# Retention followed by a maxout feed-forward layer: the attention steps of a pair of chunks one part sooner, and a queue of vector steps popped at two more places

## The chip, the cores and the metric

One core of a Trainium2 chip runs the whole program. The metric is the device time of one execution in microseconds (us), lower is better; the median of three runs is compared.

## What is computed

The kernel computes retention (attention without softmax, with a decay by distance) for 8 batches, 8 heads, 576 positions and head size 64, and feeds its output, seen as 4608 rows of 512, into a feed-forward layer whose hidden value is the largest of three products:

```python
scores = scale * np.matmul(q, k.transpose(0, 1, 3, 2))
Dmat = np.where(rel >= 0, gamma[:, None, None] ** rel[None, :, :], 0.0)
attn_out = np.matmul(scores * Dmat[None], v)
x = np.ascontiguousarray(attn_out.transpose(0, 2, 1, 3)).reshape(B * S, H * D)
h = np.maximum(np.maximum(x @ w1, x @ w2), x @ w3)      # 512 -> 768
return (h @ w_out).astype(np.float32)                    # 768 -> 512
```

All arithmetic of the matrix products is fp32. The weights arrive as 64-bit floats and are converted on the chip in the first 120 us.

## The kernel before

**Tiles and chunks.** The 4608 rows are cut into 36 chunks of 128 rows; four chunks make a tile of 512 rows, so there are nine tiles, t = 0 to 8. Retention is done chunk by chunk with a running state. While TensorE does the feed-forward layer of tile t (`ffn(t)`), the retention of the four chunks of tile t+1 is laid between its products.

**The feed-forward part.** For t of 1 and more, `up` (line 550) does one block of 128 hidden features as 20 products of 128x128 by 128x256 (`PRODUCTS`), each on a sum of blocks of x and of weights; six blocks make 120 products a tile. They gather in five PSUM chains A to E. ScalarE copies the chains to SBUF (`part`, line 564) and VectorE joins the copies (line 559), 14 joins a block. The sums of x (`X_SUMS`, 13 VectorE steps, tiles named `s`, line 344) must be there before the products that read them. Then `downs` (line 406) does seven products of six matmuls each (names `dx`, `dy`, `dz`), with four stores: after the second, fifth, sixth and seventh product. The store's tile `osb` has two buffers.

**The retention steps of a chunk g.** `load(g)` (line 199) issues 32 small DMAs for q and k in blocks of 32 and two large ones for k and v, all from SyncE's queue. `transposes(g)` (line 217) are two VectorE transposes to kT and qT. `decay_values(g)` (line 209) is one GpSimd multiply of v (tile `vd`). `scores` (line 233) is 16 matmuls, masked by two VectorE multiplies (`st`). `values([a, b], [b, next])` (line 281) is the products of the masked scores with vd, then `state` of the two chunks named second (tile `kv`, of raw k and vd), then the products with the older state; its `output` (line 320) is two VectorE multiplies into xT, and on a tile's last pair the 13 `X_SUMS`. `keep` (line 263) makes the next state, one VectorE and one GpSimd step.

**What sets the order.** The order of every engine's instructions is written out by hand. Tile t's work is cut into twelve parts: `ffn` gives way after 14, 27, 40, 54, 67, 80, 94, 107 and 120 of its 120 products, and in `downs` after the second and the fourth product and at the end. `steps(t + 1)` lists what is put ahead of part 0 to 11; a pair of chunks takes six parts, the first pair from m = 0 and the second from m = 6. TensorE and GpSimd steps stand where they are called. VectorE steps and loads go through `soon` into the deque `urgent`, from which `chore` pops one at a time: in `ffn`, after every product with an odd number within its block (lines 646 and 647), four after each product of `downs` (line 660), and all that is left at the start of `scores` and `values` and at the end of the ups. A second deque, `chores`, holds sums of weights, in t = 1 alone.

The pools that hold the loads have two buffers for the small q and k tiles and for v, three for raw k, so a load of chunk g+2 overwrites what the transposes and the decay of chunk g have read.

Of the kernel before, what the change touches and what calls it, by code (L numbers as in the profile page):

```python
# [79 lines left out]
def kernel(  # L80
# [74 lines left out]
    for r in sorted({start_of(g) for g in range(NG)} - {0, None}):  # L155
        m = masks[r] = const.tile([C, C], FP32, name=f"causal{r}")
# [17 lines left out]
    def chore(n=1):  # L174
        for _ in range(n):
            if urgent or chores:
                (urgent or chores).popleft()()  # L177
# [198 lines left out]
    def sums_of_outs():  # L376

        pool = late["pool"]
        lo, hi = slice(0, DM // 2), slice(DM // 2, DM)
        b11, b12, b21, b22 = (w_out[:, :, e, r] for e in range(2) for r in (lo, hi))  # L380
        t1, t2, t4 = (pool.tile([P, NF // 2, DM // 2], FP32, name=f"To{n}")[:] for n in (1, 2, 4))

        def on_vector(fp):
            nc.vector.tensor_tensor(t1[:, fp], b12[:, fp], b11[:, fp], op=ALU.subtract)
            nc.vector.tensor_tensor(t2[:, fp], b22[:, fp], t1[:, fp], op=ALU.subtract)

        def on_gpsimd(fp):
            nc.gpsimd.tensor_tensor(b12[:, fp], b22[:, fp], b12[:, fp], op=ALU.subtract)
            nc.gpsimd.tensor_tensor(t4[:, fp], b21[:, fp], t2[:, fp], op=ALU.subtract)

        for fp in range(NF // 2):
            chores.extend([partial(on_vector, fp), partial(on_gpsimd, fp)])
        late["T"] = {1: b11, 2: b21, 3: b22, 4: t4, 5: t1, 6: t2, 7: b12}
        late["S"] = {n: pool.tile([P, NF // 2, NH], FP32, name=f"H{n}") for n in (1, 2, 3, 4)}
# [135 lines left out]
    def weight_sums(fp):  # L530

        def step(dst, a, sign, b):
            combine(*(factor(n, slice(2 * fp, 2 * fp + 2)) for n in (dst, a, b)), sign)

        for dst, _, a, sign, b in W_SUMS:
            chores.append(partial(step, dst, a, sign, b))
        chores.append(partial(summed_fp.add, fp))

    def late_room():
        pool = late["pool"]  # L540
        late["W"] = [pool.tile([P, NF, P], FP32, name=f"n{n}") for n in range(1, 9)]
        late["X"] = {n: pool.tile([P, NH], FP32, name=n)[:] for n in sorted({x[0] for x in X_SUMS})}
# [3 lines left out]
    def convert(n):  # L546
        for _ in range(n):
            next(converting, None)
# [35 lines left out]
    def downs_plain(t, h):  # L584

        ps = [(ps_x, ps_y)[m % 2].tile([P, DM], FP32, tag="xy"[m % 2], name="down") for m in range(NT // P)]
        for fb in range(NF):
            for m, b in enumerate(ps):
                nc.tensor.matmul(b[:], lhsT=h[:, fb, m * P:(m + 1) * P], rhs=w_sb["out", fb],  # L589
                                 start=(fb == 0), stop=(fb == NF - 1))  # L590
                if fb == NF - 1:
                    osb = opool.tile([P, DM], FP32, tag="osb", name="osb")
                    nc.scalar.copy(osb[:], b[:])
                    nc.sync.dma_start(out[t * NT + m * P:t * NT + (m + 1) * P, :], osb[:])
            yield

    def up_plain(t, h, fb, i):
        ps = (ps_x, ps_y)[fb % 2].tile([P, NT], FP32, tag="xy"[fb % 2], name="up")
        for dc in range(NDC):
            nc.tensor.matmul(ps[:], lhsT=w_sb[i, fb][:, dc * P:(dc + 1) * P], rhs=xT[t][:, dc, :],  # L600
                             start=(dc == 0), stop=(dc == NDC - 1))
        if i > 0:
            return lambda: nc.vector.tensor_tensor(h[:, fb, :], h[:, fb, :], ps[:], op=ALU.max)
        return lambda: nc.scalar.copy(h[:, fb, :], ps[:])

    def ffn(t):

        h = hpool.tile([P, NF, NT], FP32, tag="h", name="h")
        if t == 0:
            for fp, i in units:  # L610
                for fb in (2 * fp, 2 * fp + 1):
                    maximum = up_plain(t, h, fb, i)
                    convert(4)
                    maximum()
                yield
            convert(6)
            for fb, _ in enumerate(downs_plain(t, h)):
                convert(4 if fb < 2 else 4 * len(pieces))
                if fb == 2:
                    while_converting.close()  # L620
                    late["pool"] = ctx.enter_context(tc.tile_pool(name="late", bufs=1))
                    late_room()
                    sums_of_outs()
                elif fb > 2:
                    chore(2)
                if fb in (1, 3):
                    yield
            yield
            return
        if t == 1:  # L630
            spread.append(True)
            weight_sums(0)
            weight_sums(2)
        plain = (2, 3) if t == 1 else ()
        order = (2, 3, 0, 1, 4, 5) if t == 1 else (0, 1, 4, 5, 2, 3)
        total = sum(24 if fb in plain else len(PRODUCTS) for fb in order)
        count = parts = 0
        for n, fb in enumerate(order):
            if fb not in plain:
                while fb // 2 not in summed_fp:  # L640
                    chore()
            steps_of_one = up_plain_all(t, h, fb) if fb in plain else up(t, h, fb)
            for step, cost in enumerate(steps_of_one):
                if fb in plain:
                    chore(8)
                elif step % 2:
                    chore(len(urgent) > 0)
                elif step % 4 == 2 and chores:
                    chores.popleft()()
                count += cost or 1  # L650
                if count * (NF // 2 * 3) >= (parts + 1) * total:
                    parts += 1
                    yield
            if n % 2:
                sums_of_hidden(h, fb // 2)
                if fb in plain:
                    weight_sums(fb // 2)
        chore(len(urgent))
        for n, _ in enumerate(downs(t, h)):
            chore(4)  # L660
            if n in (1, 3):
                yield
        yield

    def up_plain_all(t, h, fb):
        for i in range(3):
            up_plain(t, h, fb, i)()
            yield 8
# [46 lines left out]
    def steps(t):  # L715


        todo = [[] for _ in range(3 * CPT)]

        def at(n, *what):  # L720
            for step, *args in what:
                if step is values:
                    if args[0][0] < NG:
                        todo[n].append(partial(values, args[0], [g for g in args[1] if g < NG]))
                elif args[0] < NG:
                    todo[n].append(partial(soon, partial(step, *args)) if step is load else partial(step, *args))

        if t == 1:
            a, b, c, d = range(CPT, 2 * CPT)
            at(0, (load, b))  # L730
            at(1, (scores, a), (state, a), (keep, a))
            at(2, (transposes, b), (decay_values, b), (load, c))
            at(3, (scores, b), (load_blocks, d, 0))
            at(4, (decay_values, c), (load_blocks, d, 1, 2))
            at(5, (values, [a, b], [b, c]), (load_blocks, d, 3), (load, d))
            at(6, (keep, c), (transposes, c), (load_blocks, d + 1, 0))
            at(7, (transposes, d), (decay_values, d), (load_blocks, d + 1, 1, 2))
            at(8, (scores, c), (scores, d), (load_blocks, d + 1, 3), (load, d + 1))
            at(9, (load_blocks, d + 2, 0, 1))
            at(10, (decay_values, d + 1), (load_blocks, d + 2, 2))  # L740
            at(11, (values, [c, d], [d, d + 1]), (load_blocks, d + 2, 3), (load, d + 2),
               (transposes, d + 1))
            return todo
        for n in range(0, CPT, 2):
            a, b, m = CPT * t + n, CPT * t + n + 1, 6 * (n // 2)
            at(m, (keep, a), (transposes, b), (decay_values, b))
            if a == 2 * CPT:
                at(m, (load, a + 2))
            at(m, (load, b + 2))
            at(m + 2, (scores, a), (scores, b))  # L750
            at(m + 4, (decay_values, a + 2))
            at(m + 5, (values, [a, b], [b, a + 2]), (transposes, a + 2), (load, a + 4))
        return todo

    for t in range(N // NT):
# [56 lines left out]
```

## Time and profile before

| | |
|---|---|
| time, median of 3 runs | 788.36 us (788.1 to 789.76) |
| profiled run | 786.77 us, its span on the core 785.1 us |
| tile 0 with the conversion of weights | from 27.8 to about 120 us |
| tile 1 | about 120 to 211.9 us |
| tiles 2 to 7 | 82 to 84 us each; they start at 211.9, 295.4, 377.7, 461.8, 544.2 and 628.6 us |
| tile 8, without retention beside it | from 711.4 us to the end |
| granted TensorE clock | 1.00 in all stretches |

The times of a stage are read from the timeline, where each row is a run of like instructions: start, length, engine and line, output from inputs. In this trace an fp32 matmul shows as two records, so "x2" of 128x256 is one product. A row's length is the modelled busy time, which reaches into the next row; the distance between the starts of two rows is the pace.

### The profile page before, as it was taken

How to read it: one execution, taken by the hardware profiler on the slowest of the kernel's cores; microseconds unless marked ns; L12 is line 12 of the kernel's file. 1: busy time of each engine (PE TensorE's matmuls, PEld its weight loads, DVE VectorE, ACT ScalarE, POOL GpSimd, SP SyncE). 2: the span in 40 equal slices, each digit the busy share in tenths (PEclk: the TensorE clock that was granted, in tenths of full speed). 3: DMA queues.
4: the chain of work that ended last, by engine and by line, in shares of the span. 5: the costliest groups of instructions: out<-in, count | busy, mean ns of one | idle time of the engine just before them, and what ended most of it. 6: DMA issues, size and time to landing. Idle time of an engine off the chain costs nothing.

```text
span 785.1 us, 14443 instructions
## 1 busy us (share of the span) xinstructions
PE 770.2 (98%) x5000; PEld 624.6 (80%) x5000; DVE 559.6 (71%) x1248; ACT 326.2 (42%) x808; POOL 100.5 (13%) x124
## 2 busy tenths in 40 slices
PE   8999999999999999999999999999999999999998
PEld 7545454688888888888788888888888888888887
DVE  2998979989486829693877567773869296937672
ACT  3664631243154504452354325432545044524651
POOL 2110012111010211010101111110012100200000
PEclk9999999999999999999999999999999999999999
DMA  9995543323313332333333333333133423101001
GB/s 219 228 236 128 156 110 101 58 46 58 94 27 63 76 81 46 56 60 55 92 56 58 58 94 58 58 57 98 27 62 62 93 48 57 33 15 41 1 1 54
DMA packets 236937, 59.32 MB, mean 76 GB/s; under 512 B 217920, under 2 KB 235584, under 8 KB 236864
## 3 DMA queue, kind: packets, MB, share of 16 engines
q1 hardware_dynamic: 236432, 58.14, 34.5%
q8 instruction: 39, 0.64, 0.3%
q14 instruction: 34, 0.28, 0.1%
q10 hardware_dynamic: 432, 0.27, 0.1%
HBM read 48.89 MB, written 9.44 MB: 74 GB/s over the span
## 4 chain that ended last, share of the span: by engine, by line
PE 70%; DVE 12%; SPq 10%; DMA 5%; issue 2%; ACT 0%; DVEq 0%; ACTq 0%
PE a L579 13%; PE b L579 11%; SPq L195 9%; PE up L600 8%; PE dx L424 7%; PE c L579 6%; PE d L579 4%; PE e L579 3%; PE dz L424 3%; PE o L296 3%; PE s L240 3%; DVE part L559 3%; PE down L589 2%; DMA out_dram<-osb 2%; DVE s L344 2%
## 5 line engine op out<-in xcount | busy, mean ns | idle before, releaser
L559 DVE TENSOR_TENSOR part<-part 128x256 f32<-128x256 f32 x460 | 206.1, 455 | 66.2 <-ACT part L564 58.9
L564 ACT COPY part<-b 128x256 f32<-128x256 f32 x230 | 85.7, 373 | 155.4 <-PE b L579 140.2
L564 ACT COPY part<-a 128x256 f32<-128x256 f32 x276 | 102.8, 373 | 58.7 <-PE a L579 47.9
L600 PE MATMUL up<-xT,w 128*128 128x512 f32 x192 | 84.5, 595 | 0.5 <-DVE xT L184 0.5
L579 PE MATMUL b<-s,n 128*128 128x256 f32 x276 | 82.4, 380 | 1.4 <-DVE s L344 1.4
L579 PE MATMUL a<-s,w 128*128 128x256 f32 x276 | 82.2, 379 | 0.0
L600 PEld LDWEIGHTS up<-xT,w 128*128 128x128 f32 x192 | 35.8, 190 | 43.5 <-issue 40.8
L211 POOL TENSOR_TENSOR vd<-vraw,gk 128x512 f32<-128x512 f32 x36 | 38.6, 1072 | 228.5 <-DMA vraw<-in_v_dram 208.7
L441 DVE TENSOR_TENSOR osb<-dx,part 128x256 f32<-128x256 f32 x16 | 6.1, 419 | 82.2 <-PE dx L424 75.6
L579 PEld LDWEIGHTS b<-s,n 128*128 128x128 f32 x276 | 52.0, 190 | 9.9 <-ACT part L564 3.0
L579 PEld LDWEIGHTS a<-s,w 128*128 128x128 f32 x276 | 52.4, 190 | 7.2
L579 PE MATMUL c<-xT,w 128*128 128x256 f32 x184 | 56.6, 389 | 0.0
L579 PE MATMUL d<-s,w 128*128 128x256 f32 x184 | 54.8, 380 | 0.0
L579 PE MATMUL b<-xT,n 128*128 128x256 f32 x184 | 54.7, 379 | 0.0
L579 PE MATMUL e<-xT,w 128*128 128x256 f32 x184 | 47.3, 380 | 0.2 <-DVE part L559 0.2
L579 PE MATMUL a<-xT,n 128*128 128x256 f32 x184 | 47.2, 379 | 0.0
L424 PE MATMUL dx<-To,H 128*128 128x256 f32 x192 | 44.8, 383 | 0.0
L240 PEld LDWEIGHTS s<-qT,kT 64*128 64x128 f32 x576 | 34.2, 188 | 12.3 <-DVE qT L177 4.4
L559 DVE TENSOR_TENSOR h<-part 128x256 f32<-128x256 f32 x92 | 39.1, 425 | 6.6
L240 PE MATMUL s<-qT,kT 64*128 64x128 f32 x576 | 39.2, 281 | 3.3 <-DVE qT L177 3.3
L402 POOL TENSOR_TENSOR H<-h,H 128x256 f32<-128x256 f32 x24 | 18.2, 760 | 188.7 <-DVE H L401 103.6
L424 PEld LDWEIGHTS dx<-To,H 128*128 128x128 f32 x192 | 35.9, 190 | 5.7 <-issue 1.0
(104 smaller groups left out, 1286.1 us busy)
## 6 DMA issues: line engine op xcount, KB each, us to landing
bits<-in_moe_w_dram SPq DMA_DIRECT2D x36, 256.0 KB, 5.0
out_dram<-osb SPq DMA_DIRECT2D x35, 256.0 KB, 2.2
kraw<-in_k_dram SPq DMA_DIRECT2D x32, 256.0 KB, 3.0
vraw<-in_v_dram SPq DMA_DIRECT2D x32, 256.0 KB, 3.5
qraw<-in_q_dram SPq DMA_DIRECT2D x464, 16.0 KB, 1.8
kxraw<-in_k_dram SPq DMA_DIRECT2D x464, 16.0 KB, 1.8
bits<-in_moe_w_out_dram SPq DMA_DIRECT2D x6, 512.0 KB, 5.0
qraw<-in_q_dram SPq DMA_DIRECT2D x6, 256.0 KB, 5.3
```

The costliest lines, as they stand in the source:

```text
L195: nc.sync.dma_start(t[32 * a:32 * a + 32, :, blk, :], src[b, a // 2::2, pos:pos + 32, 32 * (a % 2):32 * (a % 2) + 32].rearrange("p j i -> ...
L211: nc.gpsimd.tensor_tensor(t[:], raws.pop(("v", g))[:], gk[:].unsqueeze(2).to_broadcast([C, H, D]), op=ALU.mult)
L240: nc.tensor.matmul(s[j][:, p, :], lhsT=kT[r, p, :], rhs=qT[r, p, :], start=True, stop=True)
L296: nc.tensor.matmul(o[n % 2][half(c), m, n // 2, :], lhsT=vds[g][:, h, :], rhs=sts[g][:, h % 2, h // 2, :], start=m == 0 and n < 2, stop=be ...
L344: nc.vector.tensor_tensor(dst, a, b, op=ALU.add if sign == "+" else ALU.subtract)
L402: urgent.append(lambda: (pool(s3, a11, a21, op=ALU.subtract), pool(s4, a12, s2, op=ALU.subtract)))
L424: nc.tensor.matmul(out[m], lhsT=hS[n](fp)[:, m * P:(m + 1) * P], rhs=late["T"][n][:, fp, :], start=first and fp == 0 and (m == 0 or last a ...
L559: nc.vector.tensor_tensor(out, a, b, op=op)
L564: nc.scalar.copy(t[:], ps[step[0]][:])
L579: nc.tensor.matmul(ps[chain][:], lhsT=factor(w, fb), rhs=xS[t][x], start=n == 1, stop=ends, skip_group_check=True)
L589: nc.tensor.matmul(b[:], lhsT=h[:, fb, m * P:(m + 1) * P], rhs=w_sb["out", fb], start=(fb == 0), stop=(fb == NF - 1))
L600: nc.tensor.matmul(ps[:], lhsT=w_sb[i, fb][:, dc * P:(dc + 1) * P], rhs=xT[t][:, dc, :], start=(dc == 0), stop=(dc == NDC - 1))
```

## The change

In `steps`, for all tiles but the first two, `decay_values` of the next pair's first chunk moves from part m+4 to m+3; `values`, the transposes of that chunk and the load of the chunk two further move from part m+5 to m+4. In `ffn`, a step of `urgent` is popped also after the products numbered 4 and 14 of a block of 20 (9 and 19 are odd already). At number 14 the second deque was popped before; at number 4 nothing was.

```diff
-                elif step % 2:
+                elif step % 2 or step % 5 == 4:
                     chore(len(urgent) > 0)
                 elif step % 4 == 2 and chores:
                     chores.popleft()()
...
             at(m + 2, (scores, a), (scores, b))
-            at(m + 4, (decay_values, a + 2))
-            at(m + 5, (values, [a, b], [b, a + 2]), (transposes, a + 2), (load, a + 4))
+            at(m + 3, (decay_values, a + 2))
+            at(m + 4, (values, [a, b], [b, a + 2]), (transposes, a + 2), (load, a + 4))
```

## The prediction
> **What bounds the kernel now.** First the page's line of busy times:
>
> ```profile
> PE 770.2 (98%) x5000; PEld 624.6 (80%) x5000; DVE 559.6 (71%) x1248; ACT 326.2 (42%) x808; POOL 100.5 (13%) x124
> ```
>
> TensorE (PE) is the bound, but 98% is made of modelled lengths. So I went to the timeline of PE and took distances between starts. A product in the ups takes 0.43 us (0.432 over long rows). Here are the scores of a tile's first pair (tile 3), then of its second pair:
>
> ```profile
> 307.17 1.16 PE L240 MATMUL s<-qT,kT 64*128 64x128 f32 x16
> 308.81 1.16 PE L240 MATMUL s<-qT,kT 64*128 64x128 f32 x16 [0.49 <-DVE qT L177]
> 309.91 0.70 PE L579 MATMUL c<-xT,w 128*128 128x256 f32 x2
> ...
> 348.23 2.06 PE L240 MATMUL s<-qT,kT 64*128 64x128 f32 x32
> 350.22 0.70 PE L579 MATMUL c<-xT,w 128*128 128x256 f32 x2
> ```
>
> The second pair takes 350.22 - 348.23 = 1.99 us, the first 309.91 - 307.17 = 2.74: 0.75 lost, waiting for a transpose on VectorE (DVE). The start of tile 4, PE first, then DVE:
>
> ```profile
> 380.99 0.59 PE L579 MATMUL c<-xT,w 128*128 128x256 f32 x2
> 382.19 0.67 PE L579 MATMUL b<-s,n 128*128 128x256 f32 x2 [0.60 <-DVE s L344]
> 382.70 0.59 PE L579 MATMUL a<-s,w 128*128 128x256 f32 x2
> ```
>
> ```profile
> 372.78 0.76 DVE L441 TENSOR_TENSOR osb<-dx,part 128x256 f32<-128x256 f32 x2 [10.64 <-PE dx L424]
> 373.45 1.28 DVE L177 TENSOR_TENSOR xT<-o,gq 128x512 f32<-128x512 f32 x2
> ...
> 377.78 0.76 DVE L441 TENSOR_TENSOR osb<-dz,part 128x256 f32<-128x256 f32 x2 [2.26 <-DMA out_dram<-osb]
> 378.45 0.42 DVE L344 TENSOR_TENSOR s<-xT 128x256 f32<-128x256 f32 x1
> ```
>
> 382.19 - 380.99 = 1.20, so 0.77 lost on a sum of x. DVE had stood idle for 10.64 us in the downs, then began the outputs late, and its sums stood behind an `osb` add that waited 2.26 us for a store. Last, SyncE's queue (SPq), which holds stores and loads, in two windows of the timeline, and GpSimd's (POOL) line in the list of waits:
>
> ```profile
> 373.50 0.53 SPq L207 DMA_DIRECT2D vraw<-in_v_dram  x1
> 374.12 5.39 SPq L436 DMA_DIRECT2D out_dram<-osb  x4
> ```
>
> ```profile
> 385.74 7.46 SPq L195 DMA_DIRECT2D qraw<-in_q_dram  x16
> ```
>
> ```profile
> POOL vd L211 <- DMA vraw<-in_v_dram: 208.7, 26, 22.9
> ```
>
> The queue issues four loads of about 18 us back to back (302.35 to 374.03), then four stores to 379.5, then waits to 385.74. The q transpose that frees its buffer started at 385.02 and takes 0.69: that is the wait's end.
>
> **What the Trainium skill says.** "Perfetto Trace Analysis", Identifying the Most-Contended Engine: matmul busy share does not measure the distance to the limit. The trace agrees: at 98% it still loses 0.75 us at one place. "TensorE: Matmul & The Clock Gate", Architectural detail: VectorE and ScalarE are strictly first in, first out, GpSimd per processor. The trace agrees on VectorE: the first sum started at 378.45, only after the add that had waited 2.26. "Perfetto Trace Analysis", DMA Instruction — HWDGE: a row of the issuing queue leaves out the movement of the data. So it is here: the v load's row is 0.53 us, its landing 3.5 by the page's list of issues.
>
> **The change part by part.** No instruction is added or removed; all is order.
>
> *Values of the second pair, part 11 to 10.* They now stand before the third product of the downs, 2 x 2.59 = 5.2 us sooner. Their bundle is 2 outputs, 13 sums, keep, 2 transposes, 1 load = 19 steps. Before, three products of the downs popped 4 each: 12, and 7 were left for the next tile (3 sums, keep, both transposes, load). Now five products offer 20 pops, and all 19 go before the tile ends. DVE has the room: it idles 10.64 us there. By rows (output 0.64, sum 0.42, `osb` pair 0.76, keep 0.42, transpose 0.70): the outputs and first 6 sums, 3.8 us, run while two products (5.2) run; the pair and 4 sums, 2.4, beside the next (2.6); pair, 3 sums and keep, 2.4, beside the next; two transposes, 1.4, beside the last. So the sums are there before product 8 of the next tile asks for the last one. The `osb` wait can still come, but most sums are ahead of it. The loss at each tile start (starts of rows less 0.43): tile 3 0.06; tile 4 0.18 + 0.11 + 0.77 + 0.08 = 1.14; tile 5 0.18; tile 6 0.17 + 0.11 + 0.78 + 0.07 = 1.13; tile 7 0.44; tiles 2 and 8 none. Sum **2.95 us**, all expected to go.
>
> *The first pair's transposes.* Before, the tile began with 7 leftovers plus keep, 2 transposes and load, 10 pops a block: the q transpose was the eleventh, popped at product 19, and ran at 308.06 because DVE also made up the late sums. Now only 4 stand there, popped after products 1, 3, 4, 5: the transpose is due before product 6, some 9 us ahead of scores, which follow product 27. The losses, each first-pair row less 1.99: tile 2 0.97, tile 3 0.75, tile 4 0.75, tile 5 0.75, tile 6 0.82, tile 7 0.82. Sum **4.86 us**.
>
> *Load beside it.* The transposes that freed the first load end about 379 instead of 385.71. The load then goes right behind the last store, 5 to 6 us sooner, and so do the three behind it, and the stores after those: the queue's slack. This by itself is worth nothing, PE not waiting for it, but it pays for the next step.
>
> *Values of the first pair, part 5 to 4.* Same matmuls, 13 products (5.6 us) sooner: from 327.37 to 321.76. Bound: `kv` needs vd of chunk a+2. Its multiply ran 322.56 to 323.60, as soon as v had landed. `kv` of that chunk would come 1.80 us after the values' start plus 0.28 for the chunk before, at 323.84: 0.24 to spare even with an unmoved queue, about 5.5 with the queue moved. Second pair: v issued at 355.67, landing 3.5 later, multiply done 360.2; needed at 361.1 + 2.1 = 363. I take 0, with up to 0.3 us lost in each of 6 tiles as the bad end.
>
> *Decay one part sooner.* Behind a decay that waits for v queue GpSimd's state multiplies and the two sums of hidden blocks; the downs read those sums from their fourth product on, at 363.70. With v landing by 359.2 at the latest, no one waits. 0.
>
> *Pops after 4 and 14.* After part 4 the new order on DVE is dense: two outputs 1.2 (by starts), 9 joins of products 16, 17 and 19 at 0.45 = 4.05, keep 0.42, transposes 1.4, then the next block's first join 0.45: 7.5 us from the values' end. The D chain of the next block, 20 products on, at 8.6 us, reuses the bank that this join reads: 1.1 us to spare. I take 0; bad end 0.3 a tile. In tile 1 the weight sums lose one pop a block, 4 in all; they run in the idle downs: 0.
>
> Sum: 785.1 - 2.95 - 4.86 = 777.3. For small new waits I give back 0.4 of my own choosing, so the span falls by 7.4 to 777.7. The profiled run was 786.77 and the median 788.36, so 788.36 - 7.4 = **781.0 us**.
>
> **The rivals.** *Half of it*: only the sums or only the transposes stop being waited for, since DVE stays as loaded and is first in, first out. For it: joins still wait for ScalarE often. Against: the seven leftovers go. Time: 788.36 - 2.95 = 785.4 or - 4.86 = 783.5; with both half gone, 784.5. *It does nothing*: the leftovers shift only to the middle of the tile, where the dense stretch costs as much as was saved: 788.4. For it: DVE's work is the same; against, the 1.1 us to spare. *Slower, by one mechanism*: in the dense stretch after part 4 DVE is later than I count, and the D chain waits for the bank. Four masks of 0.68, 2.7 us, running late there would eat the 1.1 and cost 1.6 in each of 7 tiles, 11.2; less 7.8 won: 791.8. It decides from 1.1 + 7.8 / 7 = 2.2 us of DVE lag more than I have. Against: the masks are popped from product 27 on, 27 products earlier.
>
> **How the numbers follow.** Forecast 0.74 (780 to 782.5), half 0.13, nothing 0.05, slower 0.08. The timed runs can tell about 0.2%, 1.6 us, from no change. Half (783.5 to 785.4) still counts as faster: 0.87 faster, 0.05 same, 0.08 slower. Low end: all 7.8 and the 1.0 us that PE loses once in tile 1 on a hidden block (149.2) gone, 779.5. High end: the bad ends of both first-pair steps together, 7 x 0.3 + 6 x 0.3 = 3.9, give 784.9.
>
> **What would show it.** Right: the row "PE s <- DVE qT" and "PE b <- DVE s" vanish; the tile starts from 2 to 8 lie 81.4 to 82.6 us apart (today's distances less the losses); `osb` waits less for stores; SPq begins a tile's first load within 1 us of the last store; GpSimd waits less for v. Wrong: PE rows after part 4 with a wait for `part` or `kv`, or scores still in two rows of 16.

## The result and the profile after

The changed kernel takes 780.15 us (median of 4 runs, 779.29 to 782.16), against 788.23 beside it (787.56 to 789.76). The ratio is 0.9898, with a 95% interval of 0.9873 to 0.9924. Forecast were 781.0 us, and a span of 777.7; the profiled span is 777.6. Timed once more beside the later experiments (runs 10 and 11), the changed kernel takes 780.89 us and the kernel before 791.75 (788.35 to 794.00). The kernel before was some 3.5 us slower there than here; no profile of it was taken there, so the reason is open, and the ratios of runs 1 to 4, 10 and 11, which are taken against it, show a larger gain than the stages do.

First, the line of busy times on the page of the changed kernel, and the lines of TensorE (PE) in its timeline that answer to the scores of tile 3 and the start of tile 4:

```profile
PE 767.2 (99%) x5000; PEld 624.4 (80%) x5000; DVE 569.7 (73%) x1248; ACT 326.0 (42%) x808; POOL 101.9 (13%) x124
```

```profile
306.34 2.06 PE L240 MATMUL s<-qT,kT 64*128 64x128 f32 x32
308.32 0.70 PE L579 MATMUL c<-xT,w 128*128 128x256 f32 x2
...
379.12 0.59 PE L579 MATMUL c<-xT,w 128*128 128x256 f32 x2
379.55 0.59 PE L579 MATMUL b<-s,n 128*128 128x256 f32 x2
379.99 0.59 PE L579 MATMUL a<-s,w 128*128 128x256 f32 x2
```

The scores stand in one row of 32, 308.32 - 306.34 = 1.98 us, where they were two rows and 2.74. The product that waited 0.77 us for a sum now follows in 0.43. Next VectorE (DVE) in the downs and into tile 4, and then SyncE's queue (SPq), from the same timeline:

```profile
363.15 1.29 DVE L177 TENSOR_TENSOR xT<-o,gq 128x512 f32<-128x512 f32 x2 [2.60 <-PE o L309]
...
371.19 0.76 DVE L441 TENSOR_TENSOR osb<-dx,part 128x256 f32<-128x256 f32 x2 [4.50 <-PE dx L424]
...
373.71 0.76 DVE L441 TENSOR_TENSOR osb<-dz,part 128x256 f32<-128x256 f32 x2 [0.18 <-PE dz L424]
...
375.17 0.42 DVE L344 TENSOR_TENSOR s<-s,xT 128x256 f32<-128x256 f32 x1
...
379.02 0.67 DVE L177 STREAM_TRANSPOSE qT<-qraw 128x512 f32<-128x512 f32 x1
```

```profile
366.49 10.86 SPq L436 DMA_DIRECT2D out_dram<-osb  x4
377.44 7.56 SPq L195 DMA_DIRECT2D qraw<-in_q_dram  x16
```

The outputs start 8 us before the output add for which they used to queue (371.19), and the last sum begins at 375.17, before tile 4 does (376.10). The adds wait for no store any more. The second q transpose runs at 379.02, 3 us into the tile; before it ran 12.7 us into tile 3, at 308.06. The queue's first load follows the last store at once, where it had waited 6 us; it now starts 1.34 us into the tile, before 8.05.

The profiled execution by stages, in us. A stage begins with the first product of a tile's 20-product blocks; the last column is what is left from there to the end.

| | to tile 1's blocks | tile 1 from there | tiles 2 to 7 | rest | span |
|---|---|---|---|---|---|
| before | 147.65 | 64.22 | 499.51 | 73.67 | 785.1 |
| after | 147.28 | 64.81 | 492.15 | 73.35 | 777.6 |

All of the gain that the change explains is in tiles 2 to 7, 7.36 us. Tile 1 lost 0.59. In tiles 4 to 7 one small wait each is new, about 0.1 us at the first product of chain d in the fourth block; run 9 comes back to it. The two outer stages differ by 0.37 and 0.32. In the last one TensorE's products of tile 8 take the same time in both; the difference lies behind its last product, where 3.6 us of the span are left before and 3.3 after. Why is not shown.

### The profile page after: what moved, and what is told of

It reads as the page before. It is cut to its first block, busy times and chain, and to the rows that moved or that the text cites. A ratio compares the mean times of both kernels' runs of the same rounds, so it can differ in the third digit from the quotient of the medians.

```text
span 777.6 us, 14439 instructions
## 1 busy us (share of the span) xinstructions
PE 767.2 (99%) x5000; PEld 624.4 (80%) x5000; DVE 569.7 (73%) x1248; ACT 326.0 (42%) x808; POOL 101.9 (13%) x124
## 4 chain that ended last, share of the span: by engine, by line
PE 84%; DVE 6%; SPq 5%; DMA 3%; issue 1%; DVEq 0%; ACT 0%
PE a L579 17%; PE b L579 15%; PE dx L424 11%; PE c L579 8%; PE dz L424 5%; PE d L579 5%; PE e L579 5%; PE up L600 5%; SPq L195 4%; PE s L240 4%; PE o L296 3%; PE dy L424 3%; PE o L309 2%; PE kv L260 2%; DMA kraw<-in_k_dram 1%
## 5 line engine op out<-in xcount | busy, mean ns | idle before, releaser
L559 DVE TENSOR_TENSOR part<-part 128x256 f32<-128x256 f32 x460 | 210.0, 465 | 77.8 <-ACT part L564 70.0
L559 DVE TENSOR_TENSOR h<-part 128x256 f32<-128x256 f32 x92 | 41.2, 448 | 6.6
L431 ACT COPY part<-dx 128x256 f32<-128x256 f32 x32 | 10.5, 375 | 80.0 <-PE dx L424 79.9
L177 DVE TENSOR_TENSOR xT<-o,gq 128x512 f32<-128x512 f32 x28 | 18.1, 686 | 33.1 <-PE o L309 33.1
L269 POOL TENSOR_TENSOR state<-state,gs 128x256 f32<-128x256 f32 x24 | 18.9, 785 | 172.9 <-DVE state L268 172.9
```

The costliest lines, as they stand in the source:

```text
L269: nc.gpsimd.tensor_tensor(t[:], t[:], gs[:], op=ALU.mult)
L559: nc.vector.tensor_tensor(out, a, b, op=op)
```

## The experiments

Theory A: the whole gain comes from the second pair, whose bundle of 19 steps is now popped inside the downs, so that neither sums nor transposes are left over. Theory B: the added pops do it. Theory C: each pair's move gives its own share, the first pair's the qT wait. The first stage varied between 147 and 151 us among runs in which it is the same, so small differences are read from the stages of the profiled executions, one for each kernel. Each time is compared with that of the kernel before that was run beside it.

**Run 1, the moves without the new pops.**

```diff
-                elif step % 2 or step % 5 == 4:
+                elif step % 2:
```

> The moves without the two new pops. Theory A (what pays is that the second pair's bundle of 19 vector steps is emptied inside the downs, so sums of x and transposes are no longer left for the next tile): both waits of TensorE go, on qT (4.86 us before) and on the sums s (2.95 us before); time within 1 us of the changed kernel, 779.5 to 781 us, and the 0.1 us waits of chain d in tiles 4 to 7 may go too, since the steps after part 4 stand less dense. Theory B (the added pops do the work): most of the gain is missing, 784 to 788 us, with the qT wait still at 0.5 to 0.7 us in six tiles.

780.99 us; the kernel before beside it took 791.71, ratio 0.9850 (0.9816 to 0.9885). Tiles 2 to 7 took 491.72 us: 7.79 less than before, where the prediction had added up 7.81 of waits. The four waits of chain d are gone. The pops are not needed for the gain; with both pairs moved, they cost 0.43 us.

**Run 2, the pops without the moves.**

```diff
-                elif step % 2:
+                elif step % 2 or step % 5 == 4:
```

(on the kernel before)

> The kernel before with pops after products 4 and 14 too. Theory A: the sums keep waiting at the tile starts (2.95 us stay), because the last sums still stand behind the store's wait; the b transposes are popped two products sooner (after 17 instead of 19), so the qT wait of 0.75 us may fall to between 0 and 0.4: 784 to 788 us. Theory B: 780 to 782 us.

786.62 us, ratio 0.9924 (0.9894 to 0.9955); tiles 2 to 7 496.90, 2.61 less than before. The qT wait is gone in all six tiles, but the tile starts got worse (4.86 - 2.61 leaves some 2.2 us more than the 2.95 lost there before). From its list of waits, TensorE's lines:

```profile
PE a L579 <- ACT osb L472: 2.0, 1, 2.0
PE b L579 <- DVE s L344: 1.6, 3, 0.6
```

Two products of lead were enough for the transposes. The sums stayed late, and in one tile ScalarE's copy stood behind a late store for so long that TensorE waited 2.0 us for it. By the stages, Theory B explains about a third of the gain, 2.61 of 7.36 us.

**Run 3, the second pair's move alone, with the pops.**

```diff
-            at(m + 3, (decay_values, a + 2))
-            at(m + 4, (values, ...), (transposes, a + 2), (load, a + 4))
+            e = n // 2
+            at(m + 4 - e, (decay_values, a + 2))
+            at(m + 5 - e, (values, ...), (transposes, a + 2), (load, a + 4))
```

> Moves of the second pair alone (part 11 to 10, 10 to 9), with the new pops; the first pair stays at parts 4 and 5. Theory A: the whole gain is here, both waits gone, and nothing is lost in tile 1 at the first feed-forward chain c (1.85 us in the changed kernel, 1.00 before) because the decay there does not move: 779 to 780.5 us, as fast as the changed kernel or up to 1 us faster. Theory C (each pair's move gives its share, the first pair's the qT wait, the second's the sums): 785 us, 2.95 us won.

780.03 us, ratio 0.9851 (0.9806 to 0.9897). Tiles 2 to 7 took 491.72 us, all of the gain and the 0.43 too; tile 1 63.70. Theory A holds for the second pair's move with the pops; C falls, since the qT wait is gone without the first pair's move.

**Run 4, the first pair's move alone, with the pops** (the same edit with `e = 1 - n // 2`).

> Moves of the first pair alone (part 5 to 4, 4 to 3), with the new pops; the second pair stays at parts 10 and 11. Theory A: no gain from the move, only what the pops give, 784 to 788.5 us; the sums wait stays at 2.95 us. The loads are not issued sooner, so vd of chunk a+2 ends just before kv reads it (0.24 us to spare by my sum): a wait of kv on vd of up to 0.5 us a tile would show. Theory C: 783.5 us, the 4.86 us of the qT wait won.

786.41 us, ratio 0.9936 (0.9909 to 0.9963), tiles 2 to 7 496.12. The sums still wait at several tile starts. And the price that the prediction had set at nothing only because the loads go out earlier shows where they don't. Its PE timeline in tile 4, and GpSimd's:

```profile
407.65 0.63 PE L260 MATMUL kv<-vd,kraw 128*64 128x64 f32 x16
409.54 0.51 PE L260 MATMUL kv<-vd,kraw 64*64 64x64 f32 x10 [1.25 <-POOL vd L211]
```

```profile
408.44 1.04 POOL L211 TENSOR_TENSOR vd<-vraw,gk 128x512 f32<-128x512 f32 x1 [19.82 <-PE kv L260]
```

`kv` waited for a vd that ended at 409.48. The row names TensorE as what the multiply waited for, but its v had been issued only from 404.43 to 405.70 and takes 3.5 us to land; in tile 3 the same row names the v load. It happened in two tiles, 0.42 and 1.25 us, 1.7 in all. The 0.24 us to spare with an unmoved queue were thus not there in these two.

**Run 5, the decay of the changed kernel put back into its old part m+4, where the values now stand.** Tile 1 had lost time mostly at one place. Lines of the changed kernel's timeline, GpSimd, VectorE and TensorE in tile 1:

```profile
146.98 1.28 POOL L211 TENSOR_TENSOR vd<-vraw,gk 128x512 f32<-128x512 f32 x1 [16.46 <-DMA vraw<-in_v_dram]
148.23 0.90 POOL L402 TENSOR_TENSOR H<-h 128x256 f32<-128x256 f32 x1
```

```profile
147.28 2.13 DVE L344 TENSOR_TENSOR n<-w,n 128x256 f32<-128x256 f32 x2
...
150.12 0.68 DVE L603 TENSOR_TENSOR h<-h,up 128x512 f32<-128x512 f32 x1
```

```profile
150.85 0.70 PE L579 MATMUL c<-s,w 128*128 128x256 f32 x2 [1.69 <-DVE h L603]
```

Two sums that took 0.75 us before take 2.13 while GpSimd multiplies and then does a hidden sum. That hidden sum ran at 138.14 before; now it stood behind the multiply, which waited for v. The maximum that frees chain c's bank (`h`, line 603) stands behind the two sums on VectorE.

```diff
-            at(m + 3, (decay_values, a + 2))
-            at(m + 4, (values, ...), (transposes, a + 2), (load, a + 4))
+            at(m + 4, (decay_values, a + 2), (values, ...), (transposes, a + 2), (load, a + 4))
```

> The changed kernel with the decay of the next pair's first chunk in the same part as the values, just ahead of them (parts 4 and 10), not a part sooner. Theory P (in tile 1 the earlier GpSimd multiply, 147.0 to 148.3, held two VectorE sums for 0.85 us each, and the plain block's maximum stood behind them): the wait of chain c falls from 1.85 back to 1.0 us, tile 1 takes about 64.0 instead of 64.8 us. Rival: the wait grew through the order of the queue or the values' move, and stays at 1.7 to 1.9. In tiles 2 to 7 nothing changes, since GpSimd waits for v's landing there and not for its turn; kv waits for vd less than 0.3 us.

The same two sums and the same wait in this run:

```profile
151.04 0.75 DVE L344 TENSOR_TENSOR n<-w,n 128x256 f32<-128x256 f32 x2
```

```profile
153.24 0.70 PE L579 MATMUL c<-s,w 128*128 128x256 f32 x2 [0.83 <-DVE h L603]
```

Tile 1 took 63.70 us instead of 64.81, tiles 2 to 7 492.14, unchanged; `kv` waited for no vd. Of the 1.11 us, 0.85 are this wait and 0.22 a wait before chain d at 167.32 in the changed kernel, which is gone too. The decay's move is what cost tile 1, and it bought nothing. (One run, 781.57 us, its first stage 150.5 us.)

**Run 6, everything one part further** (decay m+2, values, transposes and load m+3).

> Everything moved one part further still (decay m+2, values m+3). Theory A says that there is nothing left to win in tiles 2 to 7 (two waits of 0.1 us a tile at most), and that room runs out: values then stand 13 products after scores, and vd of chunk a+2 must be there 5.6 us earlier, which the queue's 5.5 us of slack just covers; 0 to 6 us longer than the changed kernel, with waits of kv on vd or o on st. Rival: moving on pays again, 1 us or more shorter.

861.1 us, about 80 more, where I had said up to 6. From its list of waits, and its timeline of SyncE's queue, ScalarE and TensorE:

```profile
PE a L579 <- ACT osb L472: 45.3, 6, 8.1
PE dx L424 <- DVE H L401: 16.6, 7, 2.9
```

```profile
202.65 7.69 SPq L195 DMA_DIRECT2D qraw<-in_q_dram  x16
...
219.14 5.40 SPq L436 DMA_DIRECT2D out_dram<-osb  x4
```

```profile
223.41 0.65 ACT L472 COPY osb<-dx 128x256 f32<-128x256 f32 x2 [15.65 <-DMA out_dram<-osb]
```

```profile
215.54 0.59 PE L579 MATMUL b<-s,n 128*128 128x256 f32 x2
224.11 1.22 PE L579 MATMUL a<-xT,w 128*128 128x256 f32 x2 [7.97 <-ACT osb L472]
```

Part 9 lies ahead of the place where `ffn` empties the deque at the end of the ups, so the whole bundle goes out at once there. Its load, 16.4 us of issues, stands ahead of all four stores of the tile, and its vector steps stand ahead of the hidden sums that the downs read. The expectation had counted landing times and neither of these orders.

**Run 7, the same with the load left in part m+5** (the edit is against run 6).

```diff
-            at(m + 3, (values, ...), (transposes, a + 2), (load, a + 4))
+            at(m + 3, (values, ...), (transposes, a + 2))
+            at(m + 5, (load, a + 4))
```

> As the run one part further, but with the load left in part m+5. In that run the queue issued a whole load of 16 us ahead of all four stores of a tile (202.65 to 219.05, stores from 219.14), since the bundle stood before the emptying of the deque at the end of the ups; ScalarE's last output copy waited 15.65 us for a store and TensorE 7 to 8 us for it. Theory L (the load ahead of the stores is what costs): the wait on the output copy (45.3 us in six tiles) and the half clock after it go; the wait of the downs on the hidden sums (16.6 us in seven tiles), which stand behind the bundle on VectorE, stays: 795 to 805 us. Rival: the bundle's vector steps delay the output copies as well, and most of the 80 us stay.

799.83 us. The wait on the output copy is gone from its list, the one on the hidden sums is the same:

```profile
PE dx L424 <- DVE H L401: 16.6, 7, 2.9
```

Tiles 2 to 7 took 571.33 us in run 6 and 511.02 here. So some 60 of the 80 us were the load ahead of the stores, with what came of it.

**Run 8, the kernel before with its stores issued by ScalarE** (`nc.scalar.dma_start` in `store`).

> The kernel before, with the stores of the downs issued from ScalarE's queue and not from SyncE's. Theory S (at the tile starts the sums of x were late because an output add ahead of them on VectorE waited for a store that stood behind a load): the waits on out_dram (8.6 us on VectorE, 22.6 on ScalarE) go, and with them the wait of the products on the sums (2.95 us down to 0.3 or less); the wait on qT (4.86 us) stays above 4. From the start of tile 2 to that of tile 8 496.5 to 497 us (before 499.5). Rival: the late start of the outputs (VectorE idle for 10.64 us behind an add that waits for TensorE) is what makes the sums late, and the loss at the tile starts stays above 2 us.

784.58 us in one run, 788.38 for the kernel before beside it. No product waited for a sum, so the store behind the load was what made the sums late. But tiles 2 to 7 took 497.41, only 2.1 less, not 2.95: the qT wait rose by 0.8 us by starts of rows. What the tile start no longer loses, the scores lose in part: the backlog on VectorE is unmoved. Moving the bundle into the downs ends both waits; whether these stores together with the pops of run 2 would do so too was not run.

**Run 9, a new pop after product 4 but not after 14.**

```diff
-                elif step % 2 or step % 5 == 4:
+                elif step % 2 or step == 4:
```

> The changed kernel with the new pop after product 4 but not after 14. The four waits of chain d (0.1 us each) and the joins before it are put down to the outputs and transposes that the pop at 14 packs into the dense stretch after part 4. Theory: without it they go, tiles 2 to 7 together 491.7 us (changed 492.15), as with the moves alone. Rival: the pop at 4 makes them, and they stay.

Tiles 2 to 7 took 491.72 us; the four waits of chain d are gone. The pop at 14 made them. (One run, 781.31 us.)

**Runs 10 and 11, a version from these findings, beside the changed kernel.** It is run 3 with seven pops instead of eight after each plain product group of tile 1, so that six sums of weights leave VectorE's backlog there.

```diff
                 if fb in plain:
-                    chore(8)
+                    chore(7)
```

> The second pair's move alone with the new pops, and seven instead of eight steps popped after each plain product group of tile 1. Theory: the wait of chain c on the hidden block in tile 1 (1.00 us with the decay unmoved, 1.85 in the changed kernel) is vector backlog from weight sums, six of which now run later; it falls below 0.3 us. From the start of the ups of tile 1 to that of tile 2 62.5 to 63 us (changed kernel 64.8), tiles 2 to 7 together 491.7 as in the second-pair run (changed 492.15): 1.5 to 2.5 us under the changed kernel. Rival: the six sums pile up ahead of the last two blocks of tile 1 and the wait only moves there: no gain over the second-pair run, 1.1 to 1.5 us under the changed kernel.

> The changed kernel itself, beside the run before it in this call: 779 to 782 us; the same waits as in its first profile (c on the hidden block 1.7 to 1.9 us, four waits of chain d of about 0.1).

The new version: 779.07 us (778.14 to 779.60, 5 runs), ratio to the kernel before 0.9842 (0.9810 to 0.9873). The changed kernel beside it: 780.89 (779.71 to 782.69, 5 runs), ratio 0.9862 (0.9830 to 0.9893). The ranges of the two don't quite meet (779.60 and 779.71), 1.8 us between the medians, though the intervals of the ratios overlap. Tile 1 took 62.53 us and tiles 2 to 7 491.72; the changed kernel again took 64.65 and 492.13. The wait of chain c is gone and did not move to the last blocks.

## Why the prediction was right

**The values of the second pair**, 2.95 us of waits on sums: right, in full. All sums are done before the next tile. Runs 1 and 3 have only this move in common and lose the waits; runs 2 and 4 lack it and keep them. The move without the pops and without the first pair's move was not run. One reading was loose: two of the 13 sums had run before the add that waited for the store (374.64 and 375.09), and eleven stood behind it.

**The first pair's transposes**, 4.86 us: the size is right. The cause given, the seven leftovers, was one of two that were each enough: the new pops alone also end the wait (run 2). With both in place neither can be seen to be needed.

**The load beside it**: the queue moved as said, by 6.7 us against the tile's start. "This by itself is worth nothing" was not run alone. That "it pays for the next step" agrees with run 4, where the queue is unmoved and `kv` waited 1.7 us in two tiles.

**Pops after 4 and 14**, "1.1 us to spare", taken as 0: this term was mis-sized. The stretch in tile 4, VectorE then TensorE:

```profile
405.48 1.29 DVE L177 TENSOR_TENSOR xT<-o,gq 128x512 f32<-128x512 f32 x2 [2.77 <-PE o L309]
407.54 1.34 DVE L559 TENSOR_TENSOR part<-part 128x256 f32<-128x256 f32 x3 [0.77 <-ACT part L564]
...
413.41 0.39 DVE L559 TENSOR_TENSOR part<-e,part 128x256 f32<-128x256 f32 x1
```

```profile
413.85 0.70 PE L579 MATMUL d<-s,w 128*128 128x256 f32 x2
414.38 0.59 PE L579 MATMUL b<-xT,n 128*128 128x256 f32 x2
```

From the start of the outputs to the end of the join, 413.80, are 8.3 us, not 7.5: my sum left out the 0.77 us in which VectorE waits for ScalarE's copy. The other side of the sum was too large: chain d follows the values by 19 products and not by 20, from 405.54 to 413.85, which is 8.3 us and not 8.6. So nothing was to spare. Chain d starts right at the join's end and loses 0.10 (0.53 to the next row). Four such waits make 0.43 us with what follows, by chance the 0.4 that I gave back of my own choosing. They are the prediction's own sign of being wrong, a product after part 4 that waits for `part`, in a small form.

**Decay one part sooner**, "0": wrong, though small. The step asked only who waits for GpSimd's results, and no one does. It named the hidden sums that queue behind the decay, but left out that the multiply, and the hidden sum after it, hold VectorE up while they run. In tile 1 that put 1.1 us on the path, and run 5 took it away.

**The sum.** Waits of 7.81 gone in tiles 2 to 7, less 0.43 for chain d, gives the 7.36 measured; tile 1 added 0.59 (1.11 lost by the decay's move, 0.52 won by the rest), and the outer stages took off 0.69 that no step explains. So 7.4 came out at 7.5 partly through terms that cancel: the waits were read rightly, the last half microsecond is luck.

**What would show it**: the two waits are gone, the tiles are 81.5 to 82.6 us apart as said, the queue starts its load at once. One sign was wrong. GpSimd waits more for v:

```profile
POOL vd L211 <- DMA vraw<-in_v_dram: 283.0, 27, 24.3
```

It was 208.7. The v load of tile 3's third chunk is issued sooner (311.67 against 318.99, 6.6 us nearer to the tile's start), but the decay stands earlier in GpSimd's own order, so more of the same wait falls to it. It costs nothing in tiles 2 to 7 (492.14 with the decay unmoved).

## What to carry to other kernels

Where the bound engine waits for a queue of small steps on another engine, count how many steps each stretch pops and where the rest falls: moving a whole bundle into a stretch in which that engine stands idle was worth 7.8 us here (runs 1 and 3), and more pops in the busy stretch were not needed. Before moving it another part, list for every queue what it then overtakes; here the bundle's load ahead of the stores cost 60 us, and its vector steps ahead of the hidden sums most of another 20.

## What the runs showed of the hardware that was not expected

A GpSimd step and a VectorE sum that both read two SBUF operands held each other up here. In the changed kernel four joins took 2.94 us beside GpSimd's two steps from 315.35 to 317.27, where four joins alone took 1.67 (at 304.25):

```profile
315.07 2.94 DVE L559 TENSOR_TENSOR part<-part 128x256 f32<-128x256 f32 x4
```
"SBUF — State Buffer", SBUF: two separate sides, says that the two engines share a port pair, that whoever starts first holds it for the whole instruction, and that a VectorE operation with two SBUF inputs is among those that need it when the GpSimd operation reads SBUF. The numbers agree in kind: beside 1.92 us of GpSimd's rows the joins took 1.27 us longer.

After a wait of 8 us TensorE comes back at half pace. In run 6 the five products from 225.12 to 229.39 took 0.85 us each by starts of rows, and those after 229.89 0.43 again; the granted clock is 0.50 from 224.11 to 229.39 and 1.00 from 229.89 on:

```profile
225.12 1.06 PE L579 MATMUL c<-s,w 128*128 128x256 f32 x2
...
229.89 0.59 PE L579 MATMUL c<-xT,w 128*128 128x256 f32 x2
```

"TensorE: Matmul & The Clock Gate", What's actually happening, describes it: the clock passes half its pulses after an idle window of about 3.4 us, until the array has been busy for about as long. Here the slow stretch lasted from 224.11 to about 229.4, 5 us, so a wait of 8 us cost nearly 3 more. A shorter wait did it too, where that window would not let one expect it. In run 7 these four products came after a wait of 2.86 us, at a clock of 0.50, and took 3.27 us to the next row instead of 1.73:

```profile
287.16 3.44 PE L424 MATMUL dx<-To,H 128*128 128x256 f32 x8 [2.86 <-DVE H L401]
```

After a wait of 2.54 us at 542.82 the clock was 0.50 again, but after one of 2.79 us at 373.17 it was 1.00, so the length of the wait alone does not decide it here.
